# A planner that holds a row store's buffer until the store has landed, with its weights chosen anew

## The chip, the cores and the metric

The kernel runs on one core of a Trainium2 chip. The metric is device time in microseconds (us) of one execution. Engines: PE (matrix products), DVE (vector), ACT (activations), POOL (GpSimd), SP (its queue issues DMAs).

## The reference, cut to what matters

Causal attention with a decay, then a mixture of experts with one expert per token, then a dense layer pair with a rational function between. 4 batches, 8 heads, 576 positions, head size 64; 2304 tokens of width 512.

```python
def _attn_ref(q, k, v, f):
    scores = scale * np.matmul(q, k.transpose(0, 1, 3, 2))
    cum = np.cumsum(np.log(np.clip(f, 0.0001, 1.0)), axis=-1)
    decay = cum[:, :, :, None] - cum[:, :, None, :]
    scores = np.where(causal, -1000000000.0, scores + decay)
    attn = np.exp(scores - np.max(scores, axis=-1, keepdims=True))
    attn = attn / (np.sum(attn, axis=-1, keepdims=True) + 1e-09)
    return np.matmul(attn, v)

def reference(**kwargs):
    attn_out = _attn_ref(**attn_kwargs)
    x = attn_out.transpose(0, 2, 1, 3).reshape(B * S, H * D)
    x = _moe_ref(x=x, **moe_kwargs)      # e = argmax(x @ w_gate); relu(x @ w1[e]) @ w2[e]
    return _moe2_ref(x=x, **moe2_kwargs)  # g = P(h) / Q(h), h = x @ w_in; g @ w_out
```

## The kernel before

Three stages follow each other: attention and the gate (until about 195 us), the experts, the dense pair. The change touches the order of the first alone.

**Attention** goes over 16 pairs of heads (4 batches of 4 pairs). For a pair, queries and keys are split into a rounded part and a rest: `kh`, `qh` by copies (lines 475 and 476; DVE and ACT), `kl`, `ql`, `q2h` on the POOL (lines 477 to 482). Then seven *steps* (line 276; step 0 to 6) each cover some heads and a tile of 128 queries: step 0 has head 0 and tile 2, step 1 head 0 and tile 3, step 2 the two tails together, step 3 head 1 and tile 3, step 4 head 1 and tile 2, steps 5 and 6 both heads with tile 1 and tile 0. A step is a chain: *scores* (PE, lines 496 and 497, tails 507 and 508; PSUM "s", 3 banks), *minimum* of the masked scores (DVE, line 519 or 531), *exponentials* with their sum (ACT, line 553 or 564), *transposes* (PE, lines 622, 626, 642; PSUM "pt", 3 banks), *move* of the transposed tile to SBUF (`move`, line 578; a copy by ACT, line 305, or DVE, line 307). When its moves are done, the *value products* of the pair follow in two parts (PE, line 665): part 0 takes the tiles from 2 on, part 1 tiles 0 and 1. A copy (`out_t`, lines 679 to 684) brings each to SBUF.

After the fourth pair of a batch, `batch` (line 689) computes the gate: sums, logits (line 760), for batches 0 to 2 transposes of the logits (line 823) and the *head sums* (`scale`, lines 827 to 836, two DVE instructions each), the choice of expert, and then five *rows*: transposes (line 926), a multiply by the DVE (`rows_m`, line 946) into a buffer "xr" (3 of them), and a store of 256 KB to `x_d`, issued by POOL (`rows_d`, lines 957 to 959). Batch 2 leaves its rows to the end, batch 3 (`b == B - 1`) has a shorter way of its own.

**What sets the order.** Each such piece is a `plan.op` (line 64) with a priority `when`, a length for each engine that may do it, what it needs, and the buffers that it takes and frees. `Plan.order` (lines 75 to 134) plays a schedule through with these lengths: at every step it finds, for each ready piece, the engine on which it ends first (the length plus `DEAR[engine]`), and on each engine takes, among those that can start within `NEAR` ns of the earliest, the one with the smallest `when`. The start times decide the order in which each engine's instructions are written; on the chip an engine does its own in that order. A buffer that a piece takes is free once the pieces that free it have ended and `reaches` (200 ns from POOL) has passed (lines 92 to 97):

```python
for u in last[k, held[k][-self.buffers[k]]]:
    if u.end is None:
        return None
    t = max(t, u.reaches(e))
```

`when` is the pair's number times `SPAN` plus a weight: `T_STEP` for the scores of each step, `T_TRANS` and `T_MOVE` for its transposes and moves, `T_LEAST` and `T_EXP` for minimum and exponentials, `T_SPLIT` and `T_SPLIT2` for the splitting, `T_PV`, `T_PV2`, `T_OUT` for the value products and their copies, `T_BATCH`, `T_BATCHJ`, `T_ROWS` for the batch (lines 279 to 284). With the two of `DEAR` and `NEAR` (lines 38 and 40) they are 31 numbers.

Of the kernel before, what the change touches and what calls it, by code (L numbers as in the profile page):

```python
# [34 lines left out]

DEAR = {"ACT": 45.9, "DVE": 316.0}

NEAR = 108.2  # L40

WARM = 6830

# [3 lines left out]
class Op:  # L47
    def __init__(self, when, lengths, emit, needs, takes, frees, shape):
        self.when, self.lengths, self.emit, self.shape = when, lengths, emit, shape
        self.needs, self.takes, self.frees = needs, takes, frees  # L50
        self.engine = self.start = self.end = None

    def reaches(self, engine):
        lat = 1000 if self.engine == "SP" else LATENCY.get((self.engine, engine), 200)
# [3 lines left out]
class Plan:  # L58
# [16 lines left out]
    def order(self):  # L75
        last = {}
        for o in self.ops:
            for b in o.frees:
                last.setdefault(b, []).append(o)
        free, held, done = {}, {k: [] for k in self.buffers}, []  # L80
        waits = {o: len(o.needs) for o in self.ops}
        shape = 0
        users = {}
        for o in self.ops:
            for n in o.needs:
                users.setdefault(n, []).append(o)
        ready = [o for o in self.ops if not waits[o]]

        def start(o, e):
            t = free.get(e, 0) + (SWITCH if e == "PE" and o.shape != shape else 0)  # L90
            t = max([t] + [n.reaches(e) for n in o.needs])
            for k in o.takes:
                if len(held[k]) >= self.buffers[k]:
                    for u in last[k, held[k][-self.buffers[k]]]:
                        if u.end is None:
                            return None
                        t = max(t, u.reaches(e))
            return t

        while ready:  # L100
            by = {}
            for o in ready:
                at = {e: start(o, e) for e in o.lengths}
                if None in at.values():
                    continue
                ends = {e: at[e] + o.lengths[e] + DEAR.get(e, 0) for e in at}
                e = min(ends, key=ends.get)
                by.setdefault(e, []).append((at[e], o))
            if not by:
                raise RuntimeError("plan stuck")  # L110
            best = None
            for e, c in by.items():
                t0 = min(t for t, _ in c)
                t, o = min((x for x in c if x[0] <= t0 + NEAR), key=lambda x: (x[1].when, x[0]))
                if best is None or t < best[0]:
                    best = t, e, o
            t, e, o = best
            n = o.lengths[e]
            if e == "PE" and t < WARM:
                n *= 2  # L120
            if e == "PE":
                shape = o.shape
            o.engine, o.start, o.end = e, t, t + n
            free[e] = o.end
            for k in o.takes:
                held[k].append(o)
            ready.remove(o)
            done.append(o)
            for u in users.get(o, ()):
                waits[u] -= 1  # L130
                if not waits[u]:
                    ready.append(u)
        assert len(done) == len(self.ops)
        return sorted(done, key=lambda o: o.start)
# [3 lines left out]
def tile_attention_moe_mlp(  # L138
# [16 lines left out]
    nc = tc.nc  # L155
# [58 lines left out]
    with ExitStack() as actx, ExitStack() as rctx:  # L214
# [61 lines left out]
        steps = [[(0, 2)], [(0, 3)], [(0, NQ)], [(1, 3)], [(1, 2)], [(0, 1), (1, 1)], [(0, 0), (1, 0)]]  # L276

        SPAN = 10000
        T_STEP = (-0.667, 0.087, 0.246, 0.842, 0.232, 0.882, 0.93)
        T_TRANS = (1.296, 0.651, 0.548, 0.123, -3.56, 0.199, -7.26)  # L280
        T_MOVE = (1.745, 0.878, 1.134, -10.074, 1.335, -2.92, 0.16)
        T_LEAST, T_EXP, T_SPLIT, T_SPLIT2 = -0.956, -0.123, 0.424, 0.017
        T_PV, T_PV2, T_OUT = -10.668, 1.768, -16.163
        T_BATCH, T_BATCHJ, T_ROWS = 0.558, 0.17, 1.464
        st = [{} for _ in range(NPAIR)]
        bt = [{} for _ in range(B)]
        rows_done, sum_ops, last_lg = [], [], []
# [401 lines left out]
        def batch(b):  # L689
# [267 lines left out]
            def rows_d(i, y, queue):  # L957
                np_ = P if i < NQ else TL
                queue.dma_start(out=x_d[b * S + i * P : b * S + i * P + np_, :], in_=y["xr"][:np_])
# [22 lines left out]
            def rows(i):  # L982
                y = {}
# [4 lines left out]
                if late:  # L988
                    o_c = plan.op(w, {"ACT": 478}, lambda e, i=i, y=y: rows_c(i, y, wt("xr", (P, DM))), [o_t], takes=["xr"], frees=[("pt", o_t)])
                    o_m = plan.op(w, {"POOL": 1210}, lambda e, i=i, y=y: rows_g(i, y), [o_c, o_g])  # L990
                    plan.op(w, {"SP": 1500}, lambda e, i=i, y=y: rows_d(i, y, nc.sync), [o_m], frees=[("xr", o_c)])
                else:
                    o_m = plan.op(w, {"DVE": 602}, lambda e, i=i, y=y: rows_m(i, y, wt("xr", (P, DM))), [o_t, o_g], takes=["xr"], frees=[("pt", o_t)])
                    rows_done.append(o_m)
                    plan.op(w, {"POOL": 1100}, lambda e, i=i, y=y: rows_d(i, y, nc.gpsimd), [o_m], frees=[("xr", o_m)])

            if late:
                return rows, rows_t, rows_a, rows_d
# [873 lines left out]
```

## Time and profile before

| what | value |
|---|---|
| median of 3 runs (lowest, highest) | 877.74 us (877.25, 879.32) |
| the profiled execution: its own time, its span | 878.83 us, 877.1 us |
| PE busy over the span, matmuls | 850.9 us (97%), 4671 |
| DVE, ACT, POOL busy | 731.0, 614.0, 350.4 us |
| between 20 and 190 us: PE, DVE, ACT busy of 170 | 165.83, 140.70, 143.64 us |
| granted TensorE clock, mean | 0.989 of 2.4 GHz |

A time in the timelines counts from the span's start. The span is what lies between the first and the last instruction; the execution's own time has 1.73 us more. Matmuls overlap: the duration of one holds the way through the array, and the next starts before it ends.

### The profile page before, as it was taken

How to read it: one execution, taken by the hardware profiler on the slowest of the kernel's cores; microseconds unless marked ns; L12 is line 12 of the kernel's file. 1: busy time of each engine (PE TensorE's matmuls, PEld its weight loads, DVE VectorE, ACT ScalarE, POOL GpSimd, SP SyncE). 2: the span in 40 equal slices, each digit the busy share in tenths (PEclk: the TensorE clock that was granted, in tenths of full speed). 3: DMA queues.
4: the chain of work that ended last, by engine and by line, in shares of the span. 5: the costliest groups of instructions: out<-in, count | busy, mean ns of one | idle time of the engine just before them, and what ended most of it. 6: DMA issues, size and time to landing. Idle time of an engine off the chain costs nothing. (4 is left out here: it accounts for less than half of the span.)

```text
span 877.1 us, 15323 instructions
## 1 busy us (share of the span) xinstructions
PE 850.9 (97%) x4671; PEld 705.9 (80%) x4671; DVE 731.0 (83%) x1400; ACT 614.0 (70%) x1267; POOL 350.4 (40%) x408
## 2 busy tenths in 40 slices
PE   7999999979999999999999999999999999999997
PEld 6777888757888887887787788999888889988885
DVE  7887989877798877888977999898898779988882
ACT  6888988874655666666536878877776667777773
POOL 8886878632132241233331233333242234223222
PEclk9999999997999999999999999999999999999999
DMA  6876769437675689688554120001000001000001
GB/s 180 194 179 150 175 174 237 158 106 245 202 248 187 194 281 302 221 307 296 179 195 145 49 72 25 29 33 37 1 37 25 13 5 56 13 1 37 1 0 49
DMA packets 49110, 110.39 MB, mean 126 GB/s; under 512 B 8419, under 2 KB 12540, under 8 KB 49018
## 3 DMA queue, kind: packets, MB, share of 16 engines
q1 hardware_dynamic: 36806, 69.70, 27.2%
q0 software_dynamic: 12208, 39.60, 13.6%
q8 instruction: 40, 0.66, 0.3%
q14 instruction: 52, 0.43, 0.2%
q10 hardware_dynamic: 4, 0.00, 0.0%
HBM read 151.85 MB, written 20.35 MB: 196 GB/s over the span
## 5 line engine op out<-in xcount | busy, mean ns | idle before, releaser
L1740 POOL TENSOR_TENSOR gl<-raw,gh 128x512 fp32r<-128x512 f32 (+1 forms) x71 | 84.4, 1189 | 206.3 <-ACT gh L1738 126.6
L1756 PE MATMUL pa<-wu,gl 128*128 128x512 f32 x256 | 100.6, 393 | 1.1 <-POOL gl L1740 1.1
L1754 PE MATMUL pa<-wu,gh 128*128 128x512 f32 x256 | 101.2, 395 | 0.0
L1755 PE MATMUL pa<-wu,gh 128*128 128x512 f32 x256 | 100.1, 391 | 0.0
L1713 ACT ACTIVATE raw<-ph 128x512 f32<-128x512 f32 (+1 forms) x80 | 44.3, 554 | 78.1 <-PE ph L1705 74.9
L1272 DVE TENSOR_TENSOR wu<-raw,wu 128x1024 fp32r<-128x1024 f32 x64 | 75.3, 1219 | 8.6 <-ACT wu L1270 6.1
L1726 DVE SCALAR_TENSOR_TENSOR raw<-raw,coef,raw 128x512 f32<-128x512 f32 (+1 forms) x80 | 66.1, 826 | 17.9 <-ACT raw L1722 15.2
L1716 DVE SCALAR_TENSOR_TENSOR raw<-raw,babs 128x512 f32<-128x512 f32 (+1 forms) x80 | 58.3, 728 | 20.8 <-ACT raw L1714 20.3
L1703 PE MATMUL ph<-colAh,wi 128*128 128x512 f32 x192 | 74.9, 390 | 0.7 <-ACTq L1644 0.7
L1705 PE MATMUL ph<-colAh,wi 128*128 128x512 f32 x192 | 74.7, 389 | 0.0
L1704 PE MATMUL ph<-colAl,wi 128*128 128x512 f32 x192 | 74.7, 389 | 0.0
L553 ACT ACTIVATE pr<-t,mn 128x384 f32<-128x384 f32 (+3 forms) x128 | 70.5, 553 | 5.0 <-DVE mn L519 3.4
L519 DVE CUSTOM_DVE_ANT_0 t<-s,mask 128x384 f32<-128x384 f32 (+3 forms) x128 | 58.3, 486 | 11.7 <-PE s L497 4.6
L1270 ACT ACTIVATE wu<-raw 128x1024 fp32r<-128x1024 f32 x64 | 64.1, 1064 | 5.2 <-DMA raw<-in_w_dram 3.5
L1727 DVE SCALAR_TENSOR_TENSOR raw<-raw,cbias 128x512 f32<-128x512 f32 (+1 forms) x80 | 57.6, 720 | 2.3
L1715 ACT ACTIVATE raw<-ph,neg 128x512 f32<-128x512 f32 (+1 forms) x80 | 59.3, 741 | 0.0
L1721 ACT ACTIVATE raw<-raw,cbias 128x512 f32<-128x512 f32 (+1 forms) x80 | 54.9, 686 | 6.3 <-DVE raw L1716 5.8
L1756 PEld LDWEIGHTS pa<-wu,gl 128*128 128x128 f32 x256 | 48.0, 188 | 12.7 <-POOL gl L1740 2.4
L1718 DVE SCALAR_TENSOR_TENSOR raw<-raw,coef,ph 128x512 f32<-128x512 f32 (+1 forms) x80 | 55.5, 693 | 2.5
L1754 PEld LDWEIGHTS pa<-wu,gh 128*128 128x128 f32 x256 | 48.1, 188 | 9.6 <-ACT gh L1738 0.8
L1755 PEld LDWEIGHTS pa<-wu,gh 128*128 128x128 f32 x256 | 48.1, 188 | 8.9
L1728 DVE SCALAR_TENSOR_TENSOR raw<-raw,raw 128x512 f32<-128x512 f32 (+1 forms) x80 | 52.4, 656 | 2.4
(296 smaller groups left out, 2387.9 us busy)
## 6 DMA issues: line engine op xcount, KB each, us to landing
raw<-in_w_dram SPq DMA_DIRECT2D x92, 1024.0 KB
rk<-in_kT_dram SPq DMA_DIRECT2D x30, 288.0 KB
rq<-in_qT_dram SPq DMA_DIRECT2D x30, 288.0 KB
d<-in_w_in_dram POOLq DMA_DIRECT2D x16, 512.0 KB
d<-in_w_out_dram POOLq DMA_DIRECT2D x16, 512.0 KB
y_d<-ys SPq DMA_DIRECT2D x22, 256.0 KB
v<-in_v_dram SPq DMA_DIRECT2D x16, 256.0 KB
wo_d<-d POOLq DMA_DIRECT2D x16, 256.0 KB
```

The lines of the kernel that those rows point to most:

```text
L553: nc.scalar.activation(u["pr"][:, sl], u["t"][:, sl], AF.Exp, bias=u["mn"][:, m : m + 1], scale=-1.0, accum_out=sm[:, i, 2 * hp + h : 2 * ...
L1270: nc.scalar.activation(w[:, 0], r, AF.Copy)
L1272: nc.vector.tensor_tensor(w[:, 1], r, w[:, 0].bitcast(F32), ALU.subtract)
L1703: nc.tensor.matmul(out_, wh, hi[:, :, c], start=(c == 0), stop=False)
L1704: nc.tensor.matmul(out_, wh, lo[:, :, c], start=False, stop=False)
L1705: nc.tensor.matmul(out_, wl_, hi[:, :, c], start=False, stop=(c == KD - 1))
L1715: nc.scalar.activation(u_, ph, AF.Identity, scale=neg[:, 3:4], bias=neg[:, 2:3])
L1726: nc.vector.scalar_tensor_tensor(u_, u_, coef[:, 0:1], rr, ALU.subtract, ALU.mult)
L1740: low.tensor_tensor(d["gl"], d["u_"], d["gh"].bitcast(F32), ALU.subtract)
L1754: nc.tensor.matmul(a_, gh[:, sl], wh, start=(m == 0), stop=False)
L1755: nc.tensor.matmul(a_, gh[:, sl], wl_, start=False, stop=False)
L1756: nc.tensor.matmul(a_, gl[:, sl], wh, start=False, stop=(m == MF - 1))
```

## The change

A piece gets a `lag`, 0 as a rule, that is added to the time at which a buffer it frees counts as free. The row stores of `rows` that POOL issues get 5000 ns, and 640 ns of POOL in place of 1100. All 31 numbers are others. No piece of work is added or taken out: 1205 pieces before and after, of which the PE has 406 in both.

```diff
-DEAR = {"ACT": 45.9, "DVE": 316.0}
+DEAR = {"ACT": 1242, "DVE": 1399}
-NEAR = 108.2
+NEAR = 20
@@ class Op
         self.engine = self.start = self.end = None
+        self.lag = 0
@@ Plan.order
-                        t = max(t, u.reaches(e))
+                        t = max(t, u.reaches(e) + u.lag)
@@ weights (a line of six)
-        T_STEP = (-0.667, 0.087, 0.246, 0.842, 0.232, 0.882, 0.93)
+        T_STEP = (-3.759, 5.896, -0.966, -23.517, -1.431, 3.105, 4.93)
...
@@ rows
-                    plan.op(w, {"POOL": 1100}, lambda e, i=i, y=y: rows_d(i, y, nc.gpsimd), [o_m], frees=[("xr", o_m)])
+                    o_d = plan.op(w, {"POOL": 640}, lambda e, i=i, y=y: rows_d(i, y, nc.gpsimd), [o_m], frees=[("xr", o_m)])
+                    o_d.lag = 5000
```

What this moves, at three places (a line number of the changed kernel is one or two higher).

**PE, the scores of step 0 of pair 6** (128x384, the second and third row in the first excerpt, the first two in the other; `s` are scores, `pt` transposes, `pr` exponentials). Before:

```order
L642 MATMUL pt<-identf,pr 128x128 x2
L496 MATMUL s<-kh,qs_108 128x384
L497 MATMUL s<-kl_112,q2s_110 128x384
L622 MATMUL pt<-identf,pr 128x128 x4
L626 MATMUL pt<-identf,pr 128x128
L642 MATMUL pt<-identf,pr 128x128 x4
L496 MATMUL s<-kh,qs_108 128x512
L497 MATMUL s<-kl_112,q2s_110 128x512
L760 MATMUL s<-ot,wl 32x320 x4
L760 MATMUL s<-ot,wl 32x256 x4
```

Now:

```order
L497 MATMUL s<-kh,qs_108 128x384
L498 MATMUL s<-kl_112,q2s_110 128x384
L497 MATMUL s<-kh,qs_108 128x512
L498 MATMUL s<-kl_112,q2s_110 128x512
L643 MATMUL pt<-identf,pr 128x128 x3
L497 MATMUL s<-kh,qs_108 128x384
L498 MATMUL s<-kl_112,q2s_110 128x384
L643 MATMUL pt<-identf,pr 128x128 x2
L508 MATMUL s<-kh,qs_108 128x288
L509 MATMUL s<-kl_112,q2s_110 128x288
```

Before, transposes of pair 5 stand behind the scores of step 0, and the transposes that belong to them come 23 rows behind these, after the logits (line 760), a value product and the scores of steps 4 and 2. Now they are the fifth row, with the scores of step 3 (128x512) alone between; the eighth row is transposes of pair 5.

**POOL, the row stores of batch 0** (`x_d`; `kl`, `qs`, `q2s` are the splitting of pairs 10 to 11 before, 9 to 11 now). Before, from the first of the five to the last:

```order
L959 DMA x_d<-xr 128x512
L460 TENSOR_TENSOR qs_108<-rq,qs_108 64x576
L470 TENSOR_SCALAR q2s_110<-rq 64x576
L959 DMA x_d<-xr 128x512
L451 TENSOR_TENSOR kl_113<-rk,kh 64x576
L747 TENSOR_SCALAR sums<-sums 128x16
L747 TENSOR_SCALAR sums<-sums 64x8
L460 TENSOR_TENSOR qs_109<-rq,qs_109 64x576
L959 DMA x_d<-xr 128x512 x2
L470 TENSOR_SCALAR q2s_111<-rq 64x576
L959 DMA x_d<-xr 64x512
```

Now, from the second of the five to the fourth:

```order
L960 DMA x_d<-xr 128x512
L471 TENSOR_SCALAR q2s_111<-rq 64x576
L960 DMA x_d<-xr 128x512
L471 TENSOR_SCALAR q2s_111<-rq 64x576
L452 TENSOR_TENSOR kl_112<-rk,kh 64x576
L730 TENSOR_TENSOR tt<-tsum 128x4
L731 COPY sums<-tt 64x4
L748 TENSOR_SCALAR sums<-sums 128x16
L461 TENSOR_TENSOR qs_108<-rq,qs_108 64x576
L960 DMA x_d<-xr 128x512
```

Before, all five stand within eleven rows, the third and the fourth directly behind each other (x2). Now one piece of splitting stands between the second and the third, six pieces between the third and the fourth, and the fifth (64x512) comes two pieces later.

**DVE, the first two head sums of batch 0** (`tmp` and `lgb`; 128x1 outputs `mn` are the read of a minimum). Before:

```order
L830 TENSOR_TENSOR tmp<-pt,rc 128x256
L834 TENSOR_REDUCE lgb<-tmp 128x32
L830 TENSOR_TENSOR tmp<-pt,rc 64x128
L834 TENSOR_REDUCE lgb<-tmp 64x16
L519 ISA t,mn<-s,mask 128x384
L519 ISA mn 128x1
L519 ISA t,mn<-s,mask 128x512
L519 ISA mn 128x1
L307 COPY pT<-pt 128x4x128
L307 COPY pT<-pt 128x4x64
L307 CAST kh<-rk 128x576 x2
```

Now:

```order
L831 TENSOR_TENSOR tmp<-pt,rc 128x256
L835 TENSOR_REDUCE lgb<-tmp 128x32
L520 ISA t,mn<-s,mask 128x384
L520 ISA mn 128x1
L831 TENSOR_TENSOR tmp<-pt,rc 64x128
L835 TENSOR_REDUCE lgb<-tmp 64x16
L532 ISA t,mn<-s,mask 128x288
L532 ISA mn 128x1
L532 ISA t,mn<-s,mask_t,mn 128x288
L532 ISA mn 128x1
L308 COPY pT<-pt 128x2x2x128
```

Before, both head sums follow each other ahead of two minima and two moves to `pT`. Now a minimum of pair 5 (128x384) stands between them, two minima of tails (128x288) follow, and the next move to `pT` is the last row.

## Rows read from the trace of the kernel before

**Rows 1.** busy times by stretch: its length, each engine's busy us and instructions.

```profile
core 0: us, PE busy (x) PEld busy (x) DVE busy (x) ACT busy (x) POOL busy (x), PEclk, DMA share, GB/s
...
20.00:190.00 170.00, 165.83 (x1368) 133.55 (x1368) 140.70 (x491) 143.64 (x456) 128.71 (x162) 1.00 0.66 170
...
205.00:877.10 672.10, 662.02 (x3133) 553.54 (x3131) 563.39 (x827) 447.55 (x759) 197.76 (x199) 1.00 0.34 112
```

**Rows 2.** waits, 20 to 190 us: who for whom, sum in us, times, longest.

```profile
POOL x_d L959 <- DVE xr L932: 3.8, 5, 1.0
...
PE pt L642 <- DVE pT L307: 2.3, 4, 1.1
...
PE pt L626 <- DVE pT L307: 1.0, 2, 0.5
```

**Rows 3.** PE's timeline: start, us, line, tiles, [idle before, releaser].

```profile
84.50 0.41 PE L642 MATMUL pt<-identf,pr 128*128 128x128 f32 x2 [1.11 <-DVE pT L307]
...
112.49 0.60 PE L622 MATMUL pt<-identf,pr 128*128 128x128 f32 x4
113.59 0.33 PE L626 MATMUL pt<-identf,pr 128*128 128x128 f32 x1 [0.50 <-DVE pT L307]
```

**Rows 4.** timeline of the DVE before the gap at 84.50.

```profile
80.87 0.42 DVE L830 TENSOR_TENSOR tmp<-pt,rc 128x256 f32<-128x256 f32 x1
...
82.30 0.37 DVE L834 TENSOR_REDUCE lgb<-tmp 64x16 f32<-64x128 f32 x1
...
83.67 1.01 DVE L307 COPY pT<-pt 128x512 f32<-128x512 f32 x2
```

**Rows 5.** timeline of the first scores to transposes, 8.5 to 12 us.

```profile
9.08 0.34 PE L497 MATMUL s<-kl,q2s 128*128 128x384 f32 x1
...
9.26 0.40 PE L496 MATMUL s<-kh,qs 128*128 128x512 f32 x1
...
9.50 0.39 PE L497 MATMUL s<-kl,q2s 128*128 128x512 f32 x1
9.57 0.56 DVE L519 CUSTOM_DVE_ANT_0 t<-s,mask 128x384 f32<-128x384 f32 x1
...
10.52 0.61 ACT L553 ACTIVATE pr<-t,mn 128x384 f32<-128x384 f32 x1
...
11.37 0.55 PE L642 MATMUL pt<-identf,pr 128*128 128x128 f32 x3 [1.19 <-ACT pr L553]
```

**Rows 6.** timeline of the ACT: the wait for pair 1's q.

```profile
16.75 0.69 ACT L457 ACTIVATE qs<-rq 128x576 fp32r<-128x576 f32 x1 [2.63 <-DMA rq<-in_qT_dram]
```

**Rows 7.** groups by form, 20 to 190 us: busy, mean, idle before.

```profile
L642 PE MATMUL pt<-identf,pr 128*128 128x128 f32 x310 | 46.8, 276 | 3.2 <-DVE pT L307 2.3 <-ACT pr L553 0.4 <-ACT pT L305 0.2
L451 POOL TENSOR_TENSOR kl<-rk,kh 64x576 fp32r<-64x576 f32 x29 | 41.6, 1436 | 6.2 <-ACT pT L305 2.2 <-PE pt L642 1.3 <-DVE kh L307 1.0
...
L642 PEld LDWEIGHTS pt<-identf,pr 128*128 128x128 f32 x310 | 35.5, 141 | 9.4 <-ACT pr L553 3.0 <-DVE pT L307 2.1 <-ACT pT L305 0.9
...
L553 ACT ACTIVATE pr<-t,mn 128x512 f32<-128x512 f32 x31 | 22.2, 716 | 2.3 <-DVE mn L519 2.2
L519 DVE CUSTOM_DVE_ANT_0 t<-s,mask 128x512 f32<-128x512 f32 x30 | 20.7, 689 | 3.2 <-PE s L497 1.5 <-ACT pr L553 1.5
L470 POOL TENSOR_SCALAR q2s<-rq 64x576 fp32r<-64x576 f32 x29 | 20.4, 705 | 2.0
...
L305 ACT ACTIVATE pT<-pt 128x512 f32<-128x512 f32 x26 | 15.3, 591 | 2.7 <-PE pt L642 2.3
L307 DVE COPY pT<-pt 128x512 f32<-128x512 f32 x21 | 14.3, 680 | 0.5 <-PE pt L642 0.5
...
L959 POOL DMA_DIRECT2D x_d<-xr x10 | 6.0, 598 | 3.8 <-DVE xr L932 3.8
```

**Rows 8.** timeline of the POOL: the first row store.

```profile
108.47 0.64 POOL L959 DMA_DIRECT2D x_d<-xr  x1 [0.53 <-DVE xr L932]
```

**Rows 9.** DMA queues between 110.4 and 111.4 us (packets, MB, share).

```profile
q0 software_dynamic: 67, 0.22, 67.7%
```

More of the change, by code (lines that the diff above doesn't have):

```diff
@@ L278, in tile_attention_moe_mlp @@
         SPAN = 10000
-        T_STEP = (-0.667, 0.087, 0.246, 0.842, 0.232, 0.882, 0.93)
[L280 to L284, printed above, removed]
+        T_STEP = (-3.759, 5.896, -0.966, -23.517, -1.431, 3.105, 4.93)
+        T_TRANS = (-11.782, -6.659, -2.002, 6.952, 0.876, -3.896, -7.853)
+        T_MOVE = (13.301, 15.853, 2.908, -1.278, 1.959, -3.062, 5.22)
+        T_LEAST, T_EXP, T_SPLIT, T_SPLIT2 = -0.419, -0.941, -0.706, -1.598
+        T_PV, T_PV2, T_OUT = -25.467, -1.585, -7.209
+        T_BATCH, T_BATCHJ, T_ROWS = -3.947, 0.307, 1.51
         st = [{} for _ in range(NPAIR)]
```

## The prediction

> **What bounds the kernel now.** I read the windows first, because the change only touches what the planner orders, and that ends near 190 us. From 205 us on nothing that the planner emits is left, and those 672 us are the same instructions in the same order [rows 1]; I cost them at nothing. So the question is one stretch. Between 20 and 190 us the PE is busy for 165.83 of 170.00 us, the DVE for 140.70 and the ACT for 143.64 [rows 1]: the PE sets the pace, and 4.17 us of idle PE is what a better order can win there. The waits of the PE come next: nearly all of that idle time is transposes (lines 642 and 626) that wait for a move of an earlier transpose, mostly by the DVE, because the three PSUM banks "pt" are taken [rows 2]. The timeline shows how large one is [rows 3]: 1.11 us at 84.50, 0.50 at 113.59. A gap is a little larger than it reads: four transposes in a row take 0.60 us [rows 3] and one 0.276 in the mean [rows 7], so they start some 0.11 apart; from the last start of the piece at 112.49 (about 112.82) to the next at 113.59 it is 0.77, so 0.66 are lost where the row says 0.50. I add 0.17 for each gap.
>
> The cause of the largest gap is on the DVE [rows 4]: at 80.87 it takes up the head sums of batch 0 (lines 830 and 834, four pieces until 82.67), then the score minima (line 519), and only at 83.67 the move that would free the bank. It is a matter of order, so the weights can mend it.
>
> **The change part by part.** *The longer hold of a store's buffer.* The old plan books 1100 ns of POOL for a row store and takes the buffer as free once that is over; the new one books 640 ns and holds the buffer 5000 ns more. The issue takes 598 ns [rows 7], so the booking is now right. The store issued at 108.47 [rows 8] still has packets in its queue after 110.4 [rows 9] (nothing else stands in that queue so early), that is 2 to 3 us after its issue, so the old hold was too short and the new one too long. No wait of the DVE for a store's landing stands in the trace; only the POOL waits, 3.8 us in five stores, for the DVE's multiply [rows 2]. Held too briefly on paper, the buffer cost nothing on the chip: 0. Its bounds are 0 and those 3.8 us, on POOL, and I take 0, since POOL is busy 128.71 of 170 us [rows 1] and no PE gap names it [rows 2]. What the hold does is spread the stores over the POOL's queue, as the second order excerpt shows.
>
> *Evacuations that change engine.* From the two built programs, 40 copies leave the ACT for the DVE and 43 go the other way. With 0.591 us on the ACT against 0.680 on the DVE for the largest [rows 7], and the smaller ones in proportion, the ACT gets some 1.7 us more and the DVE 2.1 less over 170 us: 0, since both have over 25 us free [rows 1].
>
> *The gaps that go.* The timeline has nine PE gaps in the stretch. Two lie before 40 us, where the ramp below counts, with some 0.6 of the 4.17 us; the seven after it have 3.6, and with 0.17 hidden in each, 4.8 us. In the new order the moves and the transposes that wait for them stand in other places everywhere (in the third excerpt the DVE takes other work between the head sums), so I let all seven go. **-4.8 us**; the other bound is that none goes, 0.
>
> *What is late next: the places where the new order is too tight.* I put the new PE order beside the DVE's and ACT's and looked for a step that follows its source too closely. The chain from scores to transposes is in the trace undisturbed at the start [rows 5]: the last score matmul ends at 9.42, the minimum runs 9.57 to 10.13, the exponentials 10.52 to 11.13, transposes at 11.37. The ACT was busy until shortly before 10.52; with a hop of 0.1 in place of that wait (an estimate: the hops before and after are 0.15 and 0.24) the chain is 0.15 + 0.56 + 0.1 + 0.61 + 0.24 = 1.7 us from the score matmul's end.
> - Pair 6, first excerpt: between the scores of step 0 and their transposes the new order has just the two matmuls of step 3. Such matmuls start 0.24 apart (9.26 and 9.50), and the first starts 0.16 before the end of the one ahead of it [rows 5], so the PE could begin the transposes 2 x 0.24 - 0.16 = 0.32 us after the end of step 0's scores, and their chain needs 1.7: the PE stands for about **+1.3 us**. Bounds: 0, if the scores of step 3 are late themselves (the POOL's share of the operands of pair 6), and 1.7.
> - Batch 0's head sums now stand among the scores of pair 5, with three transposes soon behind them that need the banks (third excerpt). Followed with the rows' durations, the transposes of step 3 come 0.25 too early for the ACT's move and those of step 5 of pair 4 0.35 too early for the DVE's head sum: **+0.6**. Batches 1 and 2 have the same pattern, a step looser: +0.3 each, **+0.6**. Bounds for the three together: 0 and 3 x 1.1, the largest gap of the old order [rows 3].
> - The end: the last value product of step order "1" waits for a move by the ACT, 0.591 [rows 7], plus two hops of about 0.15 and the tail 0.17; only 0.6 us of work stand between: +0.35; the logits stand one value product of 0.7 us closer to the copy that they need than before, +0.15, the hop alone. **+0.5**.
> - The ramp. Its pace is set by a load: the ACT waits until 16.75 for pair 1's q, and the scores of pair 1 need what the POOL makes of it [rows 6]. The new order does more of pair 0 before that, then lets the POOL split k twice before q, one piece of 1.44 us later. Following both to the first value product of pair 1, I find the new one behind by **+0.3**; bounds -1.2 (the PE's gap before 11.37 [rows 5]) and +1.4, that one piece [rows 7].
>
> **The sum**: -4.8 + 1.3 + 0.6 + 0.6 + 0.5 + 0.3 = -1.5 us. The profiled execution took 878.83 us, its span and 1.73 us around it, so 877.3 for one like it; the median of the three runs is 877.74, and the same difference gives **876.2 us**. About 0.3%, 2.6 us, is what a measurement of this kernel can tell from no change. So: no change that can be told.
>
> **A rule against this reading.** A matmul's weights take 0.141 us to load while transposes start 0.11 apart [rows 3, 7]; so loads overlap each other, and the sum of their times is no floor. The Trainium skill (Perfetto Trace Analysis, Identifying the Most-Contended Engine) holds the matmuls' busy share to be no good measure of the distance to the limit, since they are pipelined, and takes the share of LDWEIGHTS instead. By that the room in the stretch is 170 - 133.55 = 36 us, not 4.17, and a tighter order could bring far more than my sum; the starts that stand shoulder to shoulder in the trace speak against it.
>
> **The rivals.** *The gaps go and little comes back (faster).* The tight places of pair 6 and of the batches may be covered, since the POOL's `q2h` is booked at 1340 ns and takes 705 [rows 7], so every plan's guess of who is late is off. Then only ramp and end remain: -4.8 + 0.8 = -4.0, 873.7 us. For it: all large gaps are faults of order. Against it: pair 6 is tight by the chain's own length.
>
> *The whole order is too tight (slower).* Counting PE work between scores and their transposes pair by pair, the median lead of step 3 falls from 5.7 to 2.65 us, that of step 0 from 3.85 to 2.6. The chain of step 3 needs 0.17 + 0.15 + 0.689 + 0.1 + 0.716 + 0.15 = 2.0 us [rows 7], so 0.65 is left, about one ACT or DVE piece. It decides from the point where either engine is more than one piece behind. If both transposes are then late by 0.2 us in 15 pairs, that is +6.0 on my -1.5: 882.2 us. For it: ACT and DVE are busy 83 to 84% [rows 1], so a piece in the way is likely. Against it: the DVE and ACT orders put exactly these pieces first.
>
> *The room is larger (far faster).* If the PE could be packed to its weight loads, 36 us go. Rows 3 speak against it.
>
> **How the numbers follow.** No change that can be told 0.43; gaps go and little comes back 0.34, of which 0.02 for the larger room; too tight 0.23. Faster by over 0.3% (below 875.1) is the second, within 0.3% the first, slower (above 880.4) the third: 0.34, 0.43, 0.23. The range reaches a little past 873.7 and to the slow case: 872.8 to 882.2. The likeliest case's own range is 875.1 to 880.4.
>
> **What would show it.** In the new profile: idle PE between 20 and 190 us (4.17 now) of about 3 us; the gaps of 84.5, 113.6 and 156.5 gone; a new one of about 1.2 us between the second scores and the first transposes of pair 6; no DVE wait for a landing; the stretch after the planner unchanged. Wrong it would be if the idle PE grows through many gaps of 0.1 to 0.4 us that wait for the ACT's exponentials (too tight), or shrinks below 2 us.

## The result and the profile after

The changed kernel took **883.9 us** in the median of 5 runs (883.4 to 886.3); the kernel before, run again beside it, 879.12 (877.25 to 880.22). The ratio is 1.0054, interval 1.0031 to 1.0077: **slower by about half a per cent**, where no change that can be told had been forecast (876.2, range 872.8 to 882.2). The profiled execution took 886.30 us with a span of 884.1; that of before 878.83.

The windows of the changed kernel, with the columns of [rows 1]:

```profile
20.00:190.00 170.00, 163.80 (x1326) 132.24 (x1325) 137.56 (x477) 142.07 (x447) 124.61 (x160) 0.98 0.66 167
...
205.00:884.00 679.00, 664.90 (x3142) 555.32 (x3140) 565.74 (x829) 448.07 (x761) 200.47 (x202) 0.99 0.34 112
```

Idle PE between 20 and 190 us rose from 4.17 to 6.20 us (4.55 in the profile of a second measurement, experiment 8), and less work fits in the same 170 us: 1326 matmuls for 1368. The mean clock fell from 1.00 to 0.98 of 2.4 GHz, so in some part of the stretch it stood at the lower level of 1.2 GHz.

How much later attention ends shows at the dispatch, the first `pid` matmul. The PE's timeline of the kernel before:

```profile
196.28 1.50 PE L1240 MATMUL pid<-rs,wide 128*128 128x25 f16 x20 [5.14 <-DVE rs L1234]
```

and of the changed kernel:

```profile
200.74 1.49 PE L1242 MATMUL pid<-rs,wide 128*128 128x25 f16 x20 [5.13 <-DVE rs L1236]
```

4.46 us of the 7.47 by which the two profiled executions differ lie ahead of this row. From it to the span's end is 683.35 us where it was 680.8, 2.5 more, and the rest (0.5) lies outside the span. The largest idle times of the PE in the changed kernel between 20 and 190 us, from its timeline:

```profile
75.98 0.50 PE L497 MATMUL s<-kh,qs 128*128 128x512 f32 x1 [2.72 <-DVE mn L520]
...
129.99 0.44 PE L497 MATMUL s<-kh,qs 128*128 128x384 f32 x1 [0.81 <-DVE mn L520]
...
163.25 0.71 PE L643 MATMUL pt<-identf,pr 128*128 128x128 f32 x2 [1.90 <-ACT pr L554]
...
164.66 0.50 PE L497 MATMUL s<-kh,qs 128*128 128x512 f32 x1 [0.34 <-ACT lgs L816]
...
185.59 2.93 PE L666 MATMUL po<-pT,v 128*64 128x256 f32 x28 [0.16 <-ACT pT L306]
```

Beside these there is one of 0.28 at 163.7 to 164. None of the seven old gaps is left: no transpose waits for a move any more, where [rows 2] had 3.3 us of such waits. Three new places took their stead. Two wait for a minimum (`mn`), the third for exponentials.

**The first place** is pair 6, where +1.3 us was forecast. The DVE of the changed kernel:

```profile
71.59 0.55 DVE L308 COPY pT<-pt 128x384 f32<-128x384 f32 x1
72.06 0.19 DVE L852 TENSOR_REDUCE lmax<-lgb 128x5 f32<-128x40 f32 x1
...
73.22 0.59 DVE L308 CAST kh<-rk 128x576 fp32r<-128x576 f32 x1
73.73 0.18 DVE L855 SCALAR_TENSOR_TENSOR sc<-ex,prefs 128x40 f32<-128x40 f32 x1
73.95 0.20 DVE L858 TENSOR_REDUCE smax<-sc 128x5 f32<-128x45 f32 x1
74.19 1.35 DVE L861 TENSOR_TENSOR oh<-sc,smax 128x40 bf16<-128x40 f32 x1
75.33 0.59 DVE L520 CUSTOM_DVE_ANT_0 t<-s,mask 128x384 f32<-128x384 f32 x1
...
75.96 0.27 DVE L520 CUSTOM_DVE_ANT_0 t<-s,mask 128x128 f32<-128x128 f32 x1
```

Between 70.6 and 75.3 us the DVE does the last head sum of batch 0, its choice of expert (`lmax`, `sc`, `smax`, `oh`), copies and splitting, and no minimum. Three sets of scores wait for theirs, those of steps 6 and 1 of pair 5 and of step 0 of pair 6: the three "s" banks. So it is not the transposes of step 0 that stand but, ahead of them, the scores of step 3, which find no bank until the minimum at 75.33 is done. One instruction is out of scale: `oh`, 128x40, takes 1.35 us; all four of the kernel before took 1.4 together. The POOL beside it:

```profile
73.95 1.40 POOL L452 TENSOR_TENSOR kl<-rk,kh 64x576 fp32r<-64x576 f32 x1 [0.46 <-issue]
```

`oh` starts within this `kl` and ends 0.2 us behind it. At 127.74 it is the same, `oh` of batch 1 takes 1.28 under a `kl` from 127.39 to 128.81, and that is **the second place** (129.99).

After the first place the clock is down for some us. The windows of the changed kernel:

```profile
75.00:80.00 5.00, 4.01 (x19) 3.50 (x20) 4.54 (x19) 3.85 (x14) 4.79 (x5) 0.76 0.49 118
80.00:85.00 5.00, 5.00 (x38) 3.93 (x39) 3.93 (x17) 3.86 (x12) 2.09 (x6) 0.90 0.42 109
```

A mean of 0.76 is a mix of the two levels; the PE had stood still for 2.7 us before it fell.

**The third place.** The ACT of the changed kernel, with pair 15's `qs` copies and behind them the exponentials that the PE waits for at 163.25:

```profile
161.56 1.26 ACT L458 ACTIVATE qs<-rq 128x576 fp32r<-128x576 f32 x2 [3.79 <-POOL q2s L471]
162.72 0.39 ACT L554 ACTIVATE pr<-t,mn 128x128 f32<-128x128 f32 x1
```

and SP's queue:

```profile
150.96 2.75 SPq L409 DMA_DIRECT2D rq<-in_qT_dram  x2
```

The copies need the load of pair 15's q (`rq`), which the kernel before issued at 147.82. There the ACT waited for it too:

```profile
155.70 1.26 ACT L457 ACTIVATE qs<-rq 128x576 fp32r<-128x576 f32 x2 [3.49 <-DMA rq<-in_qT_dram]
```

In the changed kernel the profile's releaser is POOL's `q2s`, but that stands idle for the same load: in a variant that waits less, both engines' rows name it (experiment 3). Batch 1's row stores are issued from 140.30 to 148.97 (the last at 165.70), where they stood at 151.66 to 164.63; whether they make the load late is not shown, for two stores of the kernel before (151.66, 154.59) were issued while this load was under way as well.

### The profile page after: what moved, and what is told of

Its sections match the earlier page's. It is cut to its first block, busy times and chain, and to the rows that moved or that the text cites. A ratio compares the mean times of both kernels' runs of the same rounds, so it can differ in the third digit from the quotient of the medians.

```text
span 884.1 us, 15321 instructions
## 1 busy us (share of the span) xinstructions
PE 852.6 (96%) x4671; PEld 708.3 (80%) x4671; DVE 732.1 (83%) x1397; ACT 615.3 (70%) x1270; POOL 347.5 (39%) x408
## 5 line engine op out<-in xcount | busy, mean ns | idle before, releaser
L1274 DVE TENSOR_TENSOR wu<-raw,wu 128x1024 fp32r<-128x1024 f32 x64 | 75.3, 1219 | 8.8 <-ACT wu L1272 6.8
L554 ACT ACTIVATE pr<-t,mn 128x384 f32<-128x384 f32 (+3 forms) x128 | 70.6, 555 | 8.6 <-DVE mn L520 7.9
L520 DVE CUSTOM_DVE_ANT_0 t<-s,mask 128x128 f32<-128x128 f32 (+3 forms) x128 | 58.2, 485 | 11.7 <-PE s L498 7.0
L643 PE MATMUL pt<-identf,pr 128*128 128x128 f32 x320 | 49.5, 280 | 5.7 <-ACT pr L554 5.5
```

What stands on the lines that cost most here:

```text
L554: nc.scalar.activation(u["pr"][:, sl], u["t"][:, sl], AF.Exp, bias=u["mn"][:, m : m + 1], scale=-1.0, accum_out=sm[:, i, 2 * hp + h : 2 * ...
L1274: nc.vector.tensor_tensor(w[:, 1], r, w[:, 0].bitcast(F32), ALU.subtract)
```

## The experiments

In what follows a *gap* is idle time of the PE, and the *dispatch* is the start of the first `pid` matmul (196.28 before, 200.74 after) in the one profiled execution of each kernel. Medians are compared with runs of the kernel before on the same chip, 880.78, 879.42 or 879.78.

**1. The hold alone**, the old numbers kept (31 weights and the three of `DEAR` and `NEAR`, so 34 in all and not 31; `lag` in `Op` and `Plan.order` as in the change).

```diff
-plan.op(w, {"POOL": 1100}, ..., frees=[("xr", o_m)])
+o_d = plan.op(w, {"POOL": 640}, ..., frees=[("xr", o_m)])
+o_d.lag = 5000
```

> The old 31 numbers, with only the hold of 5000 ns and the 640 ns of POOL added. The order up to batch 0's first row store (108 us) is that of the kernel before. Theory (the new numbers' order costs the time, the hold costs nothing): the gaps at 62.7 and 84.5 us stay, what follows differs by gaps of at most 1 us, and the time is within 1.5 us of the kernel before. Rival (the hold is what costs, by moving stores and the work behind them): slower than before by 3 us or more, with a new gap behind 108 us.

Measured: 889.95, ratio 1.0108 (1.0086 to 1.0129), dispatch 204.85. My theory, within 1.5 us, fell; the rival's new gap behind 108 us came. The old gaps stay up to 114 us (the largest are 0.78 at 63.28, 1.11 at 85.05, 0.50 at 114.13), one of 1.83 comes at 140.63, and the gate of batch 2 is put off until behind the last logits, where nothing covers it. The PE's timeline of this kernel:

```profile
195.09 0.23 PE L1159 MATMUL ptot<-oh,onesb 128*128 128x160 bf16 x1 [1.83 <-DVE oh L861]
198.04 0.66 PE L927 MATMUL pt<-identf,ot 128*128 128x128 f32 x4 [1.34 <-ACT t L956]
204.85 1.34 PE L1242 MATMUL pid<-rs,wide 128*128 128x25 f16 x17 [6.16 <-DVE rs L1236]
```

The hold adds nothing on the chip: it changes what the planner believes, and the old numbers, chosen for another belief, give a worse order from the first store on.

**2. The new numbers alone**, without the hold (POOL 1100, no lag): experiment 1's diff the other way, on the changed kernel.

> The new 31 numbers without the hold: a store books 1100 ns of POOL and frees its buffer then. The order up to batch 0's first row store (99 us) is that of the changed kernel. Theory (the new numbers cost it): the gap of 2.7 us at 76 us and the half clock behind it stay as they are, and the time is 3 to 6 us over the kernel before. Rival (the hold makes the gaps at 130 and 163 us): those two go and nothing takes their place, so the time is 3 to 4 us under the changed kernel and within 1.5 us of the kernel before.

Measured: 891.76, ratio 1.0105 (1.0073 to 1.0138), dispatch 205.69. Both expected times fell: it is 11.0 us over the kernel before. The gap of pair 6 stays (2.71 at 76.32), so the numbers make it. And the wait that the hold is there for shows, in the DVE's timeline of this kernel:

```profile
145.87 0.69 DVE L933 TENSOR_TENSOR xr<-pt,rg 128x512 f32<-128x512 f32 x1 [2.87 <-DMA x_d<-xr]
```

and right behind it in the PE's:

```profile
146.70 0.41 PE L643 MATMUL pt<-identf,pr 128*128 128x128 f32 x2 [2.50 <-DVE xr L933]
148.12 0.87 PE L643 MATMUL pt<-identf,pr 128*128 128x128 f32 x3 [1.01 <-DVE pT L308]
```

A store at 140.28 and two from 141.30 on held all three buffers; the multiply behind them stood until one had landed, 5.6 us after the first was issued, and with it everything behind it on the DVE. Together with the new numbers the hold is worth some 5 to 6 us: without it the median lies 11.0 over the kernel before, with it 4.8 (the first measurement) and 6.0 (experiment 8), each against the kernel before on its own chip. Neither part alone is as good as the old kernel or as both.

**3. `oh` out of `kl`'s way.** From here on the order is the changed kernel's, edited by hand in `Plan.emit`: each pair of numbers puts one piece ahead of another, wherever the planner had it. Here POOL's `own_gate` (which needs `oh`) of batches 0 and 1 goes ahead of `kl` of pairs 7 and 12, so that `kl` starts after `oh`.

```diff
+MOVES = ((350, 560), (630, 928))
-        for o in self.order():
+        seq = self.order()
+        for a, b in MOVES:
+            seq.remove(self.ops[a])
+            seq.insert(seq.index(self.ops[b]), self.ops[a])
+        for o in seq:
```

> The changed kernel, with POOL's product of the chosen gate moved ahead of the split of k in batches 0 and 1, so that no split of k runs on POOL while the DVE compares for the choice of expert (oh). Theory (the DVE's compare stands still while POOL runs a product of two operands from SBUF): oh takes 0.34 us in all batches where it took 1.35 and 1.28; the gap of 2.72 us at 76 shrinks by 1.0 and the one of 0.81 at 130 goes; together 2 us less than the changed kernel, up to 3 if the clock also stays at full speed after the shorter gap. Rival (the compare is slow by itself, or waits for something else): oh still takes 1.3 us, and the time is that of the changed kernel.

Measured: 881.63, ratio 1.0017 (0.9996 to 1.0038), dispatch 196.74. The DVE of this kernel:

```profile
73.67 0.33 DVE L867 TENSOR_TENSOR oh<-sc,smax 128x40 bf16<-128x40 f32 x1
```

and its PE:

```profile
74.44 0.50 PE L503 MATMUL s<-kh,qs 128*128 128x512 f32 x1 [1.70 <-DVE mn L526]
```

`oh` takes a quarter, the gap of pair 6 shrinks by one us, and that at 130 is gone. The clock still falls (0.66 in 75 to 80 us). The dispatch is only 0.35 us earlier than in the changed kernel's repeat (197.09, experiment 8), where 1.8 us at the two places had been expected; 0.69 of the difference are the third place, of which the repeat has nothing. Its gaps here are 0.35 and 0.34, and the POOL names its cause:

```profile
156.39 1.40 POOL L477 TENSOR_SCALAR q2s<-rq 64x576 fp32r<-64x576 f32 x2 [1.85 <-DMA rq<-in_qT_dram]
```

as does the ACT:

```profile
157.56 1.26 ACT L464 ACTIVATE qs<-rq 128x576 fp32r<-128x576 f32 x2 [2.24 <-DMA rq<-in_qT_dram]
```

**4. The minima first.** The three waiting minima, with their exponentials and transposes, go ahead of batch 0's choice.

```diff
+MOVES = ((504, 463), (505, 463), (482, 346), (451, 346), (465, 349), (483, 349), (506, 349), (484, 507))
```

> The changed kernel, with the DVE's minima of pair 5's steps 6 and 1 put ahead of batch 0's choice, the minimum of pair 6's step 0 one move earlier, and the ACT's exponentials and the transposes of step 6 in the same order. Theory (the scores of pair 6's step 3 wait for a bank that minima behind the choice hold): the wait of 2.72 us of the scores goes, the transposes behind wait 0.5 to 1.5 us in its place, the clock stays full between 76 and 81 us, and the time is 2.5 to 4 us under the changed kernel. Rival (the chain from the scores of step 0 to their transposes sets the end whatever the banks do): the wait moves to the transposes at nearly its full size, over 2 us, and less than 1 us comes back.

Measured: 882.65, ratio 1.0018 (1.0001 to 1.0035), dispatch 197.43. The scores of step 3 no longer wait for a bank, which shows the cause of the 2.72. But other waits stand right behind, 2.09 us in three rows, and the dispatch is no earlier than in the repeat of the changed kernel (197.09): the rival's size came, though not by its chain.

```profile
74.58 0.49 PE L504 MATMUL s<-kl,q2s 128*128 128x512 f32 x1 [1.07 <-POOL q2s L477]
75.82 0.71 PE L649 MATMUL pt<-identf,pr 128*128 128x128 f32 x2 [0.75 <-ACT pr L560]
...
76.80 0.90 PE L649 MATMUL pt<-identf,pr 128*128 128x128 f32 x3 [0.27 <-ACT pr L560]
```

The POOL stands 2.74 us for `lmax`, which is now later, with pair 6's `q2s` behind it. The second row is the two transposes of step 6 of pair 5, whose exponentials the ACT does first. Only the third, the three transposes of step 0, is the wait that the prediction had in mind: 0.27. The clock is at 0.66 again in 75 to 80 us, where full speed had been expected.

**5. All of it at once**: experiments 3 and 4, with `q2s` and the scores of step 4 earlier, and the ACT's copies of pair 15 later (fifteen moves).

```diff
+MOVES = ((350, 560), (630, 928), (504, 558), (505, 558), ..., (530, 507), (503, 347), (1099, 892), (1104, 892), (1106, 892))
```

> The changed kernel with the edits of lock and minima together, the split of q of pair 6 on POOL ahead of its part of batch 0's choice, the scores of pair 6's step 4 ahead of the transposes of steps 6 and 0, and the ACT's copies of pair 15's q behind the exponentials of pair 13's steps 6 and 1. Theory (three places of the new order lose what the rest of it wins): the waits of the PE near 76, 130 and 163 us are under 1.2 us together, the first matmul of the dispatch (line of pid) starts at 193 to 195 us where the changed kernel has 200.7 and the one before 196.3, and the time is 5 to 7 us under the changed kernel and 1.5 to 3 under the one before. Rival (each wait only moves on to the next source): pid at 197 or later, no faster than the kernel before.

Measured: 880.76, ratio 1.0021 (1.0002 to 1.0039), dispatch 196.78. Pair 6 keeps one gap of 1.06, ahead of the three transposes of step 0, after which the clock stays at 1.00; but 0.86 come at 84.88 (for `q2s`) and 1.34 at 163.31 (for a move by the DVE). The rival, that waits only move on, held in the main; its dispatch, 197 or later, was missed by 0.2.

**6. The clock by itself.** 40 matmuls of constants, into a bank whose result nobody reads, stand behind the scores of step 0 of pair 6 (piece 504) and fill the gap.

```diff
             o.emit(o.engine)
+            if o is self.ops[504]:
+                self.busy()
...
+        def busy():
+            ps = bank(ps_o, "po")
+            for _ in range(40):
+                nc.tensor.matmul(ps[:, :P], onesb, after, start=True, stop=True)
+
+        plan.busy = busy
```

> The changed kernel with 40 extra products of constants on the PE behind the scores of pair 6's step 0 (2.2 us at 56 ns each, in the 2.7 us in which the PE waits there); their result is not used. Theory (half of what the place costs is the lower clock that follows the idle PE): the wait that is left is 0.3 to 0.6 us, the scores of step 3 start when they did, the granted clock between 76 and 81 us is 1.00 where it was 0.5 until 80.7, and the dispatch starts 1.5 to 2 us sooner than in the changed kernel. Rival (the clock falls whatever the PE does there): clock and times stay.

Measured: 880.81, ratio 1.0014 (0.9996 to 1.0031), dispatch 196.18. The scores of step 3 start at 76.02 with the filling and at 75.98 without; the clock of the window behind them, with the columns of [rows 1]:

```profile
75.00:80.00 5.00, 4.52 (x38) 3.79 (x36) 4.91 (x20) 4.00 (x14) 4.85 (x5) 1.00 0.53 126
```

From there to the gap at 129 to 130 it is 52.5 us, 54.0 in the changed kernel and 53.6 in its repeat: the lower clock costs 1.1 to 1.5 us beside the gap itself.

**7. The load earlier**: pair 15's q load ahead of an earlier one of pair 14, and one load of expert weights (`raw`) behind.

```diff
+MOVES = ((1186, 1187), (1095, 1037))
```

> The changed kernel with the load of pair 15's q ahead of pair 14's values and the second of four loads of expert weights (1 MB) behind it. Theory (the ACT's and POOL's wait near 160 us is for this load, which shares the DMA engines with that megabyte): the load lands 2 us sooner or more, the PE's wait of 1.90 us at 163 falls under 0.4 us, and the dispatch starts up to 2.5 us sooner. Rival (the wait is for POOL's own order): it stays at 1.5 us or more.

Measured: 881.53, ratio 1.0022 (1.0006 to 1.0038), dispatch 197.64; the issue moves from 150.96 to 146.60, and nothing is left of the gaps at 163. Its median lies 3.9 us under that of the changed kernel on the same chip (experiment 8). That is no measure of the load alone: the edits of experiments 3, 4 and 6 do not move it, and their medians too lie only 0.9, 1.9 and 1.4 us over the kernel before, with at most 0.35 us left of the 1.90 at 163. And experiment 7 moves two loads at once, so it does not tell which one counts.

**8. The changed kernel again**, unedited.

> The changed kernel once more, unaltered, beside the others on their chip. Theory: the wait of 2.72 us at 76 and the one of 0.81 at 130 belong to the order and come again within 0.1 us; the one at 163 depends on a load and comes with another size, between 0 and 2 us; the time is 3 to 6 us over the kernel before.

Measured: 885.38, ratio 1.005 (1.0023 to 1.0076). Its seven runs fall into two groups, 880.0 to 882.0 (three) and 885.4 to 888.3 (four). The profiled one is of the lower group (881.96), dispatch 197.09: the gaps of pair 6 (2.72) and of 129.39 (0.80) are the same, but there is none at 163. SP's row there:

```profile
150.36 1.37 SPq L409 DMA_DIRECT2D rq<-in_qT_dram  x2
```

0.6 us earlier and 1.37 long, where it was 2.75. The POOL, which waits for the load, goes on at 155.85, 5.5 us after the issue; in the first profile it goes on at 160.09, 9.1 us after. So the third place comes in some executions only: 56.09 us from the gap at 129 to the last logits here, 59.15 in the first profile. Why the load took longer there was not found. That it parts the two groups of times fits both profiles, but only one of each kind was taken, and the five runs of the first measurement (883.4 to 886.3) do not fall into these groups.

**9. The best of these together**: experiments 3 and 7, and 24 matmuls of constants at pair 6 and as many behind pair 0's last scores.

```diff
+MOVES = ((350, 560), (630, 928), (1186, 1187), (1095, 1037))
+            if o in (self.ops[142], self.ops[504]):
+                self.busy(24)
```

> The changed kernel with the edits of lock and of load, and 24 products of constants in each of two waits of the PE (behind the last scores of pair 0 and behind the scores of pair 6's step 0). Theory (the places add up, each at the size measured alone): against the changed kernel without its wait for pair 15's load (dispatch at 197.1) 1.0 at pair 6, 0.8 at 130, 1.1 to 1.5 for the clock behind pair 6 and about 1 for the clock behind 17 us go: dispatch at 192.8 to 193.6, the kernel before had 196.3, and the time is 2 to 3.5 us under the kernel before. Rival (what is taken away at one place comes back at the next): dispatch at 195.5 or later, no faster than the kernel before.

Measured: 879.98, ratio 0.9995 (0.998 to 1.0009), the same as before, where 2 to 3.5 us less had been expected. Its dispatch is at 193.94, 2.3 us earlier than before and near the 192.8 to 193.6 expected, and the largest waits left behind 12 us are 0.35 at pair 6 and 0.32 at 21. But the span ends at 878.9, and what follows the dispatch is 4.2 us longer than before. The experts wait, in the PE's timeline, where the kernel before has 0.32 and 0.19 at these two places:

```profile
329.41 0.66 PE L1491 MATMUL px<-identf,h 128*128 128x128 f32 x4 [1.18 <-ACT h L1484]
...
342.53 1.11 PE L1491 MATMUL px<-identf,h 128*128 128x128 f32 x4 [2.37 <-ACTq L1354]
```

These two are 3.0 of the 4.2 us.

**10. The kernel before with its first gap filled** by 22 matmuls of constants.

```diff
+            if o is self.ops[90]:
+                self.busy(22)
```

> The kernel before with 22 products of constants on the PE ahead of its first transposes, in the 1.2 us in which it waits for the first exponentials. Theory (the half clock from 12 to 15 us follows that wait): the clock stays full there, scores of 128x288 start 0.13 apart where they start 0.24, and up to 1 us comes back before 17 us; from there the wait for pair 1's load takes it again, so that the dispatch is 0 to 0.5 us sooner. Rival (the clock is not set by that wait): it falls as before, and the products only push the first transposes by up to 0.2 us.

Measured: 881.27, ratio 1.0018 (1.0002 to 1.0034). The clock of 12 to 16 us rises from 0.61 to 1.00, but the PE then waits 1.60 us for exponentials at 18.93 (0.53 at 18.09 before), and the clock is at 0.50 from 20 to 23. The dispatch is at 197.51, 1.2 us later than before, and not sooner; 1.0 of it lies ahead of the edit, for the first scores start at 9.80 in this execution (8.80 before). The ACT waits for pair 1's q until 17.60 here (16.75 in [rows 6]): a faster PE only waits longer.

**11 and 12. The kernel before and that of experiment 9, once more.**

> The kernel before, unaltered, for a second profile. Theory (the experts' waits for weights, 135 and 147 us behind the dispatch, come with another size in each execution, whatever the order of the attention): the dispatch starts within 0.5 us of 196.3, and what follows it takes anything from 680 to 685 us, where the first profile had 680.8. Rival (the new order is what makes the experts wait): what follows the dispatch takes 680.8 within 0.5.

> The kernel of best, unaltered, for a second profile. Theory (as for the kernel before): the dispatch starts within 0.5 us of 193.9, and what follows takes anything from 680 to 685 us, where the first profile had 685.0. Rival (an attention stage that ends sooner waits for the experts' weights): what follows takes 685 within 0.5, so that the gain of 2.3 us at the dispatch is always given back.

Measured: 878.72 (dispatch 196.40, 680.6 from there to the span's end) and 877.84 (193.70, 682.2), beside one run of the kernel before of 879.79. The earlier dispatch is there again, 2.7 us; the experts' wait some 135 us behind it, 2.44 here, is 1.49 in the kernel before. Over all the profiles this wait lies between 0.3 and 3.6 us, in the first changed profile at 2.75, which is the 2.5 us that it lost behind the dispatch. What follows the dispatch came out the same in both profiles of the kernel before, 680.8 and 680.6, as the rival for it had; in those of the other it is 685.0 and 682.2, so its rival fell. Whether an earlier end of attention makes the wait longer, or it only varies, was not settled.

## Why the prediction was wrong

The step that failed is "What is late next": it followed single chains from scores to transposes and had no term for banks that minima hold, for the lower clock behind a gap, or for a late load; and the stretch behind the planner was put at nothing. The runs show some 4.2 us at pair 6 for the +1.3, and, in the first profile, 3.1 for the load and 2.5 behind the dispatch. The cause of the 4.2 is shown (experiments 3, 4 and 6); what makes the load and the experts' weights late stays open.

**The gaps that go: right.** All seven went, 4.7 us with what was hidden in them, for the 4.8 of the sum.

**Pair 6, +1.3: the wrong mechanism, and too small.** The step followed one chain, from the scores of step 0 to their own transposes, and gave each hop its own length. Once the banks were free, the transposes of step 0 waited only 0.27 (experiment 4) and 1.06 (experiment 5). What stopped the PE ahead of them were the banks: the prediction did not count who holds the three "s" banks, though it had done so for "pt". The minima that would free them stand behind batch 0's choice (experiment 4), which is made 1 us longer by the POOL (experiment 3). The rows of the kernel before could have warned: [rows 7] gives `kl` 1.436 us, and nobody asked what the DVE does beneath one. Then comes the lower clock, 1.1 to 1.5 us (experiment 6), which no step of the prediction had. In place of +1.3 stand +2.88, from one start to where the next would have been, and some 1.3.

**The batches, +0.6 and +0.6: wrong places.** No gap stands at batch 0's head sums. In batch 1 it is the choice again, +0.8.

**The hold at 0: wrong as a part, right for its wait.** In the kernel before no multiply waits for a landing; in the new order without the hold one does, 2.87 us, and in the first profile of the changed kernel one still waits 1.1 (none in the repeat). "The new one too long" was read from one store, 2 to 3 us from issue to landing; the four large stores of batch 1 in the repeat (KB each, median us from issue to landing) took longer in the median than the hold's 640 + 5000 ns:

```profile
x_d<-xr POOLq DMA_DIRECT2D x4, 256.0 KB, 6.8
```

An edit to a planner has no price of its own: on the old numbers the same hold costs 9 us (experiment 1), on the new it saves 5 to 6 (experiment 2).

**What was not priced at all: the loads.** The prediction looked at the orders of PE, DVE, ACT and POOL, and "spreads the stores" was all that it said of them. It did not ask when the loads land: pair 15's q, for which the ACT of the kernel before waited 3.49 us, is issued 3.1 us later. That is the third place, 1.90 + 0.28 + 0.34 = 2.5 us in gaps (3.1 by the stretch from 129 to the logits, experiment 8), and it comes in some executions only. That the stores, 11 us earlier in batch 1, delay it was not tested.

**The end, +0.5, and the ramp, +0.3.** The end measured 0.16 (its own terms add up to 0.46 + 0.15 = 0.6, and not 0.5). For the ramp the sum leaves about +0.5, which no row shows by itself. That sum, against the profile of the repeat, which has no third place: -4.7 + 2.88 + 1.2 + 0.8 + 0.16 = +0.3, and its dispatch is later by 0.81. With the third place, 3.1, and 0.6 more ahead of it (the gap of 129 stands at 129.99 there, at 129.39 in the repeat), the first profile's 4.46 comes out.

**The signs that the prediction named.** Idle PE was to be about 3 us and is 6.20 (4.55 in the repeat); the new gap of pair 6 was to lie between the second scores and the transposes and lies ahead of the second scores; no multiply was to wait for a landing and one does in the first profile, 1.1; and the stretch behind the planner was to stay, but its wait for weights makes it 2.5 longer.

**The rivals.** "Too tight" had the sign and nearly the size (882.2), but by many waits of 0.1 to 0.4 us; there are three large places and few small ones. "Little comes back" fell. Of the larger room nothing was seen: with nearly all gaps closed (experiment 9) the dispatch gains 2.3 to 2.7 us, not 36. The Trainium skill (Perfetto Trace Analysis, Identifying the Most-Contended Engine) goes by the share of weight loads. It is 132.24 of 170 us in the slower kernel, 133.55 in the faster, and 136.50 in experiment 9, where the PE stands idle for 2.3: by that rule some 33 us of room are left there. No run here packed the PE tighter, so this room is neither seen nor disproved.

## What to carry to other kernels

Where a generated order changes, follow every pool of buffers, not only the chain of one step: list who holds each bank at the moment when the next taker comes, and on which engine the releasers queue. Follow the DMA queues as well: a load that is issued just in time can land late in some executions (5.5 and 9.1 us here). And price a planner's rule only together with the numbers chosen for it: each half of this change alone cost 9 us or more, both together 5 to 6.

## What the hardware showed

**A DVE instruction can stand beneath one of the POOL.** `oh` compares two operands in SBUF. It takes 0.34 us in all four cases of the kernel before, and 1.35 and 1.28 where it starts within a `kl` of the POOL, also from two operands in SBUF; `kl` itself takes 1.40 and 1.42 there, and 1.44 in the mean before [rows 7]. Moved out of its way `oh` takes 0.33 (experiment 3). In batch 2 of the changed kernel it takes 0.65 and ends 0.2 us behind a POOL cast of 173.45 to 174.05. The Trainium skill (SBUF — State Buffer, Who interferes with whom) says just this: a VectorE instruction with two SBUF inputs contends with a GpSimd instruction that reads SBUF, and issue order decides who blocks. By that rule `oh`, which starts second, waits for `kl`; the traces agree: it ends at 74.19 + 1.35 = 75.54, `kl` at 73.95 + 1.40 = 75.35, and at the second place they end at 129.02 and 128.81.

**A gap can cost more than its length, and need not.** Behind 2.72 us the clock went to its lower level for 3.4 us (by the two windows under the first place), and also behind 1.70 (experiment 3) and behind 1.07 and 0.75 close together (experiment 4), but not behind one of 1.06 (experiment 5) nor where matmuls of constants filled the time (experiment 6). The length of the gap does not decide it: behind the 1.90 us at 163.25 the first profile of the changed kernel shows full speed (columns of [rows 1]),

```profile
163.00:168.00 5.00, 4.35 (x29) 3.69 (x30) 3.00 (x12) 4.63 (x16) 4.59 (x7) 1.00 0.74 241
```

and behind 2.23 us at 17.75 it is at the lower level,

```profile
20.00:23.00 3.00, 3.00 (x11) 2.09 (x10) 1.90 (x7) 2.63 (x10) 2.45 (x3) 0.50 1.05 238
```

where its repeat, behind 2.13 us at 17.66, is not:

```profile
20.00:23.00 3.00, 2.69 (x18) 1.80 (x19) 1.35 (x5) 2.92 (x12) 2.52 (x3) 1.00 1.01 252
```

What else decides was not found here.

**One load, early or late.** The same load of pair 15's q is in time in one execution of the changed kernel and late in another, and this accounts for 3 us between the two profiles. The seven runs of experiment 8 lie in two groups about 5 us apart; the five of the first measurement do not, so that the load makes the groups is not shown.
